# Attention and expert layer on one core: small VectorE steps that read at most one SBUF operand, and three kinds of work moved to other engines

## The chip, the cores and the metric

The kernel runs on one core of a Trainium2 chip. The core has TensorE (PE, matrix multiplication), VectorE (DVE), ScalarE (ACT), GpSimd (POOL) and SyncE (SP, which here only issues transfers), a working memory SBUF, and PSUM, into which TensorE writes. The metric is the device time of one execution in microseconds (us).

## What is computed

Sparse softmax attention, followed by a layer of eight experts, in float32. Per head, scores below the row's maximum minus tau are dropped. Each token then goes to the expert with the largest logit, up to a capacity per expert.

```
q, k, v: (4 batches, 8 heads, 576, 64);  w_gate: (512, 8);  w1: (8, 512, 1024);  w2: (8, 1024, 512)

scores = q @ k^T / 8
scores = where(scores >= max(scores) - tau, scores, -1e9)
attn   = exp(scores - max(scores));  attn /= sum(attn) + 1e-9
x      = concat of the heads of (attn @ v)              # (2304, 512)

logits = x @ w_gate;  e = argmax(logits);  gate_w = softmax(logits)[e]
out[i] = gate_w[i] * relu(x[i] @ w1[e]) @ w2[e]         # while expert e has room (576 tokens)
```

## The kernel before

Two heads make a pair; there are 16 pairs, four per batch. A head has 576 rows: four blocks of 128 and a tail of 64. Products need more than f16 gives, so q, k, v and the probabilities are split into an f16 high half and an f16 low half (the rest), and the products of halves are added up in PSUM.

For one pair, the stages are these, with the names that the profile shows for the tiles:

- Loads of q, k and v go to `qr`, `kr` and `v`. ScalarE scales q and k in place (L704, from the third pair on). `emit_hi` (L710, ScalarE) writes the high half into `qn` or `kn`; `emit_dup` (L714, VectorE) copies it to a second place of the same tile; `emit_lo` (L721, GpSimd; in the first two pairs VectorE) writes the low half. A transposing transfer makes `qT` and `kT` of them (L743, L748).
- v is scaled in place by GpSimd (`emit_vs`, L729); ScalarE makes the high half `vH` (L732) and GpSimd the low half `vL` (L735).
- Score pass: TensorE writes scores into two PSUM tiles `s` in turn (L761), and VectorE takes the row maximum of each (`emit_max`, L788, L790, L794) into `mx`. A score matmul waits until the maximum of the tile two before is taken.
- Threshold: `emit_m` (L799 to L804, six VectorE steps on 128x9 elements) makes of the maxima the two columns of `qn` that carry the row's threshold. A transposing transfer of `qn` follows (L753).
- Second pass: TensorE computes the transposed scores less the threshold into two PSUM tiles `d` (L761); ScalarE takes the exponential (L846), and VectorE multiplies it by "score is at or above the limit" (`emit_keep`, L850). The result lies in a part of the buffers that the profile names `w1b` and `w2b`.
- Of the five tiles per pair four are split into halves `p`: high by ScalarE (`emit_h16`, L816), low by `emit_l16` (L820). Of these four, tile 4 is VectorE's (`BY_V = {4}`) and the other three are GpSimd's.
- Output: TensorE multiplies the probabilities by v into the PSUM tile `xo` (`emit_av`, L866, L878); a column of constants in v gives the row sums in the same product. `xo` holds one head at a time in columns 0 to 259, and the tail rows behind them. ScalarE copies it to `xs` (`emit_xe`, L893); VectorE adds 1e-9 to the sums (`emit_r`, L899) and takes the reciprocal `rc` (L900); GpSimd multiplies (`emit_xm`, L914). The next head's output matmuls wait for `emit_xe`.
- After the fourth pair of a batch come transposes, logits, the choice of expert and scatters of the rows to DRAM. When all pairs are through, the expert part loads the weights, splits them into halves, and multiplies.

`ps_g`, which the profile names `gp`, is one PSUM bank that several small results share: transposed rows in columns 0 to 255, logits and ranks behind them, two 64-wide tail products at 320 and 384.

The order of the instructions is not the order of the text. Each step is a task with an engine, a duration, its dependencies and a due time (`T(name, engine, duration, function, dependencies, due)`), and a planner places the tasks one after the other on each engine by these durations and due times; each engine then runs its list in order. The due times are offsets to the pair's number (`PR`). The planner's duration of `emit_m`, for example, is 600 ns, and that of `emit_l16` 2350 ns on GpSimd and 1130 ns on VectorE.

## Time and profile before

| | |
|---|---|
| median of 3 runs | 714.22 us (709.1 to 725.44) |
| the profiled execution | 712.3 us, span 710.4 us |
| busy: TensorE / VectorE / ScalarE / GpSimd | 584.7 / 530.8 / 339.1 / 333.1 us |
| attention up to about 422 us, expert part behind | |
| granted TensorE clock, middle of the attention (120 to 340 us) | 0.90 of full |

An instruction's busy time runs from its start to its end, so it holds whatever the instruction itself waits for after it has begun. Idle time before an instruction is put down to the event that released it. Matmuls overlap each other, so a busy TensorE is not one at its peak.

### The profile page before, as it was taken

What the parts mean: (1) busy time and instruction counts of PE and PEld (TensorE: products, weight loads), DVE (VectorE), ACT (ScalarE), POOL (GpSimd) and SP (SyncE); (2) the same over time, 40 slices, a digit from 0 to 9 for tenths busy, and PEclk for the clock granted to TensorE, in tenths of its full rate; (3) what the DMA queues carried; (4) which work ended last, traced back from release to release, by engine and by line L of the source; (5) the groups of instructions that cost most, each with busy time, mean ns of one, the idle gap of its engine ahead of it and who ended that gap; (6) DMA issues with size and microseconds to landing.
All of it is one profiled execution on the core that took longest, in us unless ns stands there. A gap on an engine that the chain in (4) does not pass through costs nothing.

```text
span 710.4 us, 15942 instructions
## 1 busy us (share of the span) xinstructions
PE 584.7 (82%) x5990; PEld 389.1 (55%) x5990; DVE 530.8 (75%) x989; ACT 339.1 (48%) x535; POOL 333.1 (47%) x323
## 2 busy tenths in 40 slices
PE   0668877797798888878976886689999699899993
PEld 0225644575556665545744683577586268558741
DVE  5678988979999989999799767755456557686552
ACT  2347565546556655555344745446664206324300
...
GB/s 159 178 164 119 118 118 89 80 118 147 90 116 109 135 79 133 101 88 65 51 77 52 212 120 214 176 247 107 315 266 182 222 64 152 176 245 79 140 189 83
DMA packets 172428, 98.97 MB, mean 139 GB/s; under 512 B 147123, under 2 KB 159479, under 8 KB 172346
## 3 DMA queue, kind: packets, MB, share of 16 engines
...
q10 hardware_dynamic: 1296, 0.89, 0.4%
...
## 4 chain that ended last, share of the span: by engine, by line
PE 30%; DVE 30%; DMA 15%; issue 13%; POOL 4%; ACT 4%; SPq 3%; POOLq 0%; ACTq 0%; DVEq 0%
DVE w2b L850 7%; DVE mx L788 6%; DMA ws<-in_moe_w_dram 5%; PE s L761 5%; PE xo L866 4%; PE d L761 4%; PE b L370 4%; DVE rc L899 3%; PE b L377 3%; PE gp L930 2%; PE b L413 2%; PE gp L413 2%; POOL out_dram L602 2%; DMA latey<-xd,gix 2%; PE xo L413 2%
## 5 line engine op out<-in xcount | busy, mean ns | idle before, releaser
L761 PE MATMUL s<-kT,qT 128*128 128x512 f16 (+2 forms) x576 | 108.7, 330 | 67.5 <-DVE mx L788 46.5
L850 DVE SCALAR_TENSOR_TENSOR w2b<-d,ntau,w2b 128x1024 f32<-128x1024 f32 x80 | 101.8, 1273 | 9.0 <-ACT w2b L846 8.9
L788 DVE TENSOR_REDUCE mx<-s 128x1 f32<-128x512 f32 x144 | 95.0, 677 | 16.5 <-PE s L761 16.1
L294 POOL DMA_DIRECT2D ws<-in_moe_w_dram x50 | 36.9, 738 | 148.9 <-DVE w1b L307 68.7
L761 PEld LDWEIGHTS <-qT 128*128 128x128 f16 (+1 forms) x640 | 41.0, 108 | 98.9 <-issue 71.3
L846 ACT ACTIVATE w2b<-d 128x1024 f32<-128x1024 f32 x80 | 79.9, 1020 | 31.0 <-PE d L761 30.1
L761 PE MATMUL d<-qT,kT 128*128 128x512 f16 (+2 forms) x576 | 88.0, 317 | 6.6 <-DVE w2b L850 6.1
L377 PE MATMUL b<-w1b,latex 128*128 (+2 forms) x816 | 80.6, 277 | 5.1 <-issue 5.0
L820 POOL TENSOR_TENSOR p<-w2b,p 128x1024 f16<-128x1024 f32 x31 | 66.1, 2134 | 27.9 <-ACT p L816 27.5
L377 PEld LDWEIGHTS <-latex 128*128 128x128 f16 (+1 forms) x816 | 63.2, 102 | 20.4 <-issue 4.2
L761 PEld LDWEIGHTS <-kT 128*128 128x128 f16 (+1 forms) x640 | 39.6, 107 | 50.8 <-issue 27.4
L866 PE MATMUL xo<-v,w2b 128*128 128x65 f32 x256 | 56.5, 304 | 0.0
L816 ACT ACTIVATE p<-w2b 128x1024 f16<-128x1024 f32 x42 | 44.2, 1052 | 24.8 <-DVE w2b L850 24.5
L413 PEld LDWEIGHTS <-lateh 128*128 128x128 f16 (+1 forms) x408 | 31.3, 105 | 42.2 <-issue 10.7
L307 DVE SCALAR_TENSOR_TENSOR w2b<-ws,w2b 128x1024 f16<-128x1024 f32 (+1 forms) x40 | 39.5, 1006 | 19.1 <-ACT w2b L305 16.6
L370 PEld LDWEIGHTS <-w1b 128*128 128x128 f16 x768 | 46.6, 102 | 9.1 <-issue 7.6
L370 PE MATMUL b<-earlyx,w1b 128*128 128x128 f16 x768 | 49.9, 225 | 1.7 <-DVE earlyx L352 1.6
L866 PEld LDWEIGHTS <-p 128*128 128x128 f16 x1008 | 45.3, 104 | 10.4 <-issue 2.5
L307 DVE SCALAR_TENSOR_TENSOR w1b<-ws,w1b 128x1024 f16<-128x1024 f32 (+1 forms) x40 | 40.0, 1007 | 12.0 <-ACT w1b L305 12.0
L866 PE MATMUL xo<-vH,p 128*128 128x65 f16 x672 | 48.2, 201 | 0.1
L305 ACT ACTIVATE w2b<-ws 128x1024 f16<-128x1024 f32 (+1 forms) x40 | 34.3, 880 | 25.6 <-DMA ws<-in_moe_w_dram 23.8
L305 ACT ACTIVATE w1b<-ws 128x1024 f16<-128x1024 f32 (+1 forms) x40 | 34.1, 882 | 25.4 <-DMA ws<-in_moe_w_dram 25.4
...
## 6 DMA issues: line engine op xcount, KB each, us to landing
...
```

Of the source, the lines that this page charges most:

```text
L305: nc.scalar.activation(out=dst[:, :, 0, :], in_=t, func=AF.Copy, scale=W_SCALE)
L307: nc.vector.scalar_tensor_tensor(out=dst[:, :, 1, :], in0=t, scalar=W_SCALE, in1=dst[:, :, 0, :], op0=ALU.mult, op1=ALU.subtract)
L370: nc.tensor.matmul(out=hp[:, f * P:(f + 1) * P], lhsT=wb[0][:, o:o + P], rhs=xT[t][:, xi], start=(d == 0 and z == 0), stop=(d == NB - 1 an ...
L377: nc.tensor.matmul(out=hp[m, 0:FC], lhsT=xT[t][:, xi, m], rhs=wb[0][:, bass.ds(r + (2 * d + wi) * FC, FC)], start=(d == 0 and z == 0), sto ...
L413: nc.tensor.matmul(out=yp[m], lhsT=h[:, o, hi, m], rhs=wb[1][:, bass.ds(r + wi * DM, DM)], start=(z == 0), stop=(z == len(ops) - 1),)
L761: nc.tensor.matmul(out=out, lhsT=l, rhs=r, start=(z == 0), stop=(z == 1), **kw)
L788: V.tensor_reduce(out=m[:, 0, i:i + 1], in_=ps_s[i % 2], axis=AX.X, op=ALU.max)
L816: nc.scalar.activation(out=p16_of(s, k)[:, 0], in_=p32_of(s, k), func=AF.Copy)
L820: eng.tensor_tensor(out=p[:, 1], in0=p32_of(s, k), in1=p[:, 0], op=ALU.subtract)
L846: nc.scalar.activation(out=t, in_=d, func=AF.Exp, scale=sc_s)
L850: V.scalar_tensor_tensor(out=t, in0=d, scalar=ntau, in1=t, op0=ALU.is_ge, op1=ALU.mult)
L866: nc.tensor.matmul(out=ps_x[:, j * DV:j * DV + r.shape[-1]], lhsT=l, rhs=r, start=(z == 0), stop=(z == len(ops) - 1))
```

## The change

The maxima of a pair go to a tile of another layout: `mx` is now `[P, KB, 2]` (KB = 9), with the two maxima of a row side by side, and one reduction over the last axis takes the place of the elementwise maximum. It is done twice, once into PSUM (`a`) and once into SBUF (`m`, in the new tile `mm`). The following steps keep their intermediate values in PSUM, in 27 columns of `ps_g` from column 448 on (54 with the next pair), so that each step has at most one tensor operand in SBUF. `emit_r` reads the row sums from the PSUM tile `xo` instead of from `xs`. `emit_dup` is gone: `emit_hi` writes both places in one ScalarE instruction that reads its input twice. The scaling of v moves from GpSimd to ScalarE. The low half of tile 4 moves from VectorE to GpSimd. The tasks' durations and dependencies follow; the due times are the same.

```diff
-        mxs = [right.tile([P, 4, KB], F32, name=f"mx{i}") for i in range(2)]
+        mxs = [right.tile([P, KB, 2], F32, name=f"mx{i}") for i in range(2)]
+        mms = [right.tile([P, KB], F32, name=f"mm{i}") for i in range(2)]
...
-            nc.scalar.activation(out=n[:, 0, :, 0:D], in_=raw, func=AF.Copy, scale=sc)
-
-        def emit_dup(s, is_q):
-            n = qns[s % NQN] if is_q else kns[s % NKN]
-            V.tensor_copy(out=n[:, 1, :, 0:D] if is_q else n[:, 0, :, D:], in_=n[:, 0, :, 0:D])
+            out = view(n[:, 0, 0], [[KB * P if is_q else D, 2], [P, KB], [1, D]])
+            src = view(raw[:, 0], [[0, 2], [D, KB], [1, D]])
+            nc.scalar.activation(out=out, in_=src, func=AF.Copy, scale=sc)
...
-            nc.gpsimd.tensor_scalar(out=v, in0=v, scalar1=QK_SCALE, scalar2=None, op0=ALU.mult)
+            nc.scalar.activation(out=v, in_=v, func=AF.Copy, scale=QK_SCALE)
...
-                V.tensor_reduce(out=m[:, 0, i:i + 1], in_=ps_s[i % 2], axis=AX.X, op=ALU.max)
+                V.tensor_reduce(out=m[:, i, 0:1], in_=ps_s[i % 2], axis=AX.X, op=ALU.max)
...
-            m, n = mxs[s % 2], qns[s % NQN]
-            V.tensor_tensor(out=m[:, 2], in0=m[:, 0], in1=m[:, 1], op=ALU.max)
-            V.scalar_tensor_tensor(out=m[:, 3], in0=m[:, 2], scalar=-1.0, in1=m[:, 2], op0=ALU.mult, op1=ALU.max)
-            V.tensor_scalar(out=m[:, 3], in0=m[:, 3], scalar1=ROUND, scalar2=ntau, op0=ALU.mult, op1=ALU.add)
-            V.scalar_tensor_tensor(out=m[:, 3], in0=m[:, 3], scalar=0.0, in1=m[:, 2], op0=ALU.max, op1=ALU.subtract)
-            V.tensor_scalar(out=n[:, 1, :, D], in0=m[:, 3], scalar1=1.0 / MC, scalar2=None, op0=ALU.mult)
+            m, n = mms[s % 2], qns[s % NQN]
+            o = CM + s % 2 * 3 * KB
+            a, w, g = (ps_g[:, o + i * KB:o + (i + 1) * KB] for i in range(3))
+            for out in (a, m):
+                V.tensor_reduce(out=out, in_=mxs[s % 2], axis=AX.X, op=ALU.max)
+            V.scalar_tensor_tensor(out=w, in0=a, scalar=-1.0, in1=m, op0=ALU.mult, op1=ALU.max)
+            V.tensor_scalar(out=w, in0=w, scalar1=ROUND, scalar2=ntau, op0=ALU.mult, op1=ALU.add)
+            V.scalar_tensor_tensor(out=g, in0=w, scalar=0.0, in1=m, op0=ALU.max, op1=ALU.subtract)
+            V.tensor_scalar(out=n[:, 1, :, D], in0=g, scalar1=1.0 / MC, scalar2=None, op0=ALU.mult)
             V.scalar_tensor_tensor(
-                out=n[:, 1, :, D + 1], in0=n[:, 1, :, D], scalar=-MC, in1=m[:, 3], op0=ALU.mult, op1=ALU.add
+                out=n[:, 1, :, D + 1], in0=n[:, 1, :, D], scalar=-MC, in1=g, op0=ALU.mult, op1=ALU.add
             )
...
-            V.tensor_scalar(out=r0, in0=t[:, :, D:], scalar1=1e-9 * QK_SCALE, scalar2=None, op0=ALU.add)
+            sums = ps_x[rows, o:o + n * DV].rearrange("p (j d) -> p j d", d=DV)[:, :, D:]
+            V.tensor_scalar(out=r0, in0=sums, scalar1=1e-9 * QK_SCALE, scalar2=None, op0=ALU.add)
...
-        BY_V = {4}
+        BY_V = set()
...
-                T(("hi" + n, s), "A", 660, partial(emit_hi, s, is_q, scaled), got + free, u + PR["hi"] + is_q)
-                T(("du" + n, s), "V", 220, partial(emit_dup, s, is_q), [("hi" + n, s)], u + PR["lo"] + is_q)
+                T(("hi" + n, s), "A", 1170, partial(emit_hi, s, is_q, scaled), got + free, u + PR["hi"] + is_q)
...
-            T(("vs", s), "G", 1800, partial(emit_vs, s), [("lv", s)], u + PR["vs"])
+            T(("vs", s), "A", 760, partial(emit_vs, s), [("lv", s)], u + PR["vs"])
...
-                        need += [("xe", s, 0)] if x == 1 else last("xe", s - 1, 1 if x == 0 else 2)
+                        need += [(m, s, 0) for m in ("xe", "r")] if x == 1 else last("xe", s - 1, 1 if x == 0 else 2) + last("r", s - 1, 1 if x == 0 else 2)
...
-                T(("r", s, x), "V", 200, partial(emit_r, s, x), [("xe", s, x)], t1 + PR["xe"])
+                T(("r", s, x), "V", 200, partial(emit_r, s, x), [("av", s, x, j) for j in js], t1 + PR["xe"])
```

The first place in the order is VectorE's list around the threshold chain of one pair in the middle of the attention. Before, it reads (`s_144` and `s_145` are the two score tiles, `rc_192` the row sums of the second head):

```order
L794 TENSOR_REDUCE mx_186<-gp 128x1
L899 TENSOR_SCALAR rc_192<-xs_189 128x4
L900 RECIPROCAL rc_192<-rc_192 128x4
L799 TENSOR_TENSOR mx_186<-mx_186 128x9
L800 SCALAR_TENSOR_TENSOR mx_186<-mx_186 128x9
L801 TENSOR_SCALAR mx_186<-mx_186,ntau 128x9
L802 SCALAR_TENSOR_TENSOR mx_186<-mx_186 128x9
L803 TENSOR_SCALAR qn_178<-mx_186 128x9
L804 SCALAR_TENSOR_TENSOR qn_178<-qn_178,mx_186 128x9
L788 TENSOR_REDUCE mx_187<-s_144 128x1
L788 TENSOR_REDUCE mx_187<-s_145 128x1
L714 COPY kn_175<-kn_175 128x9x64
```

The same place of the changed kernel, whose lines are numbered a little differently (L801 to L806 are the chain, L852 is `emit_keep`, L903 the row-sum step):

```order
L793 TENSOR_REDUCE mx_186<-gp 128x1
L801 TENSOR_REDUCE gp<-mx_186 128x9
L801 TENSOR_REDUCE mm_188<-mx_186 128x9
L802 SCALAR_TENSOR_TENSOR gp<-gp,mm_188 128x9
L803 TENSOR_SCALAR gp<-gp,ntau 128x9
L804 SCALAR_TENSOR_TENSOR gp<-gp,mm_188 128x9
L805 TENSOR_SCALAR qn_178<-gp 128x9
L806 SCALAR_TENSOR_TENSOR qn_178<-qn_178,gp 128x9
L852 SCALAR_TENSOR_TENSOR w2b<-d_146,ntau,w2b 128x1024
L852 SCALAR_TENSOR_TENSOR w2b<-d_147,ntau,w2b 128x1024
L903 TENSOR_SCALAR rc_194<-xo 128x4
L904 RECIPROCAL rc_194<-rc_194 128x4
```

The chain has seven rows instead of six, the copy behind it is gone, and the row-sum step, which now reads `xo`, stands behind two large steps instead of ahead of the chain.

The second place is ScalarE's list at about the same time. Before (`w2b<-d` is the exponential, `p` and `w1b<-w2b` the high half of probabilities):

```order
L846 ACTIVATE w2b<-d_146 128x1024
L816 ACTIVATE p_157<-w2b 128x1024
L924 ACTIVATE w1b<-gp 128x256
L704 ACTIVATE kr_171<-kr_171 128x576
L924 ACTIVATE w1b<-gp 128x256
L816 ACTIVATE p_158<-w2b 128x1024
L846 ACTIVATE w2b<-d_147 128x1024
L846 ACTIVATE w2b<-gp 128x64
L710 ACTIVATE qn_178<-qr_173 128x9x64
L710 ACTIVATE kn_176<-kr_172 128x9x64
```

And in the changed kernel (L728 is the scaling of v, L713 the doubled copy, L848 the exponential, L818 the high half):

```order
L848 ACTIVATE w2b<-d_147 128x1024
L728 ACTIVATE v_167<-v_167 128x10x64
L713 ACTIVATE kn_175<-kr_171 128x2x9x64
L895 ACTIVATE xs_190<-xo 128x260
L818 ACTIVATE w1b<-w2b 128x1024
L848 ACTIVATE w2b<-d_146 128x1024
L848 ACTIVATE w2b<-d_147 128x1024
L713 ACTIVATE qn_177<-qr_174 128x18x64
L818 ACTIVATE w1b<-w2b 128x1024
```

The scaling of v, which waits for its load, and two instructions of twice the size now stand between the exponentials.

## Rows read from the trace of the kernel before

**Rows 1.** Page, 40 equal slices: span, busy tenths of TensorE and VectorE.
```profile
span 710.4 us, 15942 instructions
...
PE   0668877797798888878976886689999699899993
...
DVE  5678988979999989999799767755456557686552
```

**Rows 2.** Busy time by stretch: PE, PEld, DVE, ACT, POOL, clock, DMA, GB/s.
```profile
120.00:340.00 220.00, 186.83 (x2139) 127.00 (x2137) 205.24 (x365) 124.50 (x186) 135.03 (x110) 0.90 0.56 107
...
422.00:710.00 288.00, 252.81 (x2238) 167.57 (x2237) 169.75 (x314) 112.08 (x193) 82.72 (x95) 0.93 0.71 176
```

**Rows 3.** Waits, 120 to 340 us: total us, times, longest.
```profile
PE s L761 <- DVE mx L788: 28.9, 19, 3.4
```

**Rows 4.** Timeline of VectorE: start us, duration us; pairs 3 and 13.
```profile
91.56 0.14 DVE L799 TENSOR_TENSOR mx<-mx 128x9 f32<-128x9 f32 x1
...
327.03 0.14 DVE L799 TENSOR_TENSOR mx<-mx 128x9 f32<-128x9 f32 x1
```

**Rows 5.** Timeline of VectorE, 187 to 193 us.
```profile
187.18 1.27 DVE L850 SCALAR_TENSOR_TENSOR w2b<-d,ntau,w2b 128x1024 f32<-128x1024 f32 x1
...
188.50 0.89 DVE L899 TENSOR_SCALAR rc<-xs 128x4 f32<-128x4 f32 x1
...
190.72 2.09 DVE L803 TENSOR_SCALAR qn<-mx 128x9 f16<-128x9 f32 x1
```

**Rows 6.** Timeline of GpSimd, the same stretch.
```profile
187.23 2.13 POOL L820 TENSOR_TENSOR w1b<-w2b,w1b 128x1024 f16<-128x1024 f32 x1 [0.29 <-ACT w1b L816]
...
190.64 2.12 POOL L820 TENSOR_TENSOR w1b<-w2b,w1b 128x1024 f16<-128x1024 f32 x1
```

**Rows 7.** Groups of VectorE: busy us, mean ns; idle before.
```profile
L799 DVE TENSOR_TENSOR mx<-mx 128x9 f32<-128x9 f32 x16 | 6.0, 373 | 0.0
L800 DVE SCALAR_TENSOR_TENSOR mx<-mx 128x9 f32<-128x9 f32 x16 | 4.6, 286 | 0.6
L801 DVE TENSOR_SCALAR mx<-mx,ntau 128x9 f32<-128x9 f32 x16 | 9.7, 608 | 0.6
L802 DVE SCALAR_TENSOR_TENSOR mx<-mx 128x9 f32<-128x9 f32 x16 | 10.6, 660 | 0.6
L803 DVE TENSOR_SCALAR qn<-mx 128x9 f16<-128x9 f32 x16 | 9.9, 617 | 0.8 <-DMA kr<-in_k_dram 0.3
L804 DVE SCALAR_TENSOR_TENSOR qn<-qn,mx 128x9 f16<-128x9 f16 x16 | 10.5, 659 | 0.5
L899 DVE TENSOR_SCALAR rc<-xs 128x4 f32<-128x4 f32 (+1 forms) x48 | 30.8, 642 | 8.0 <-ACT xs L893 7.6
L714 DVE COPY qn<-qn 128x576 f16<-128x576 f16 x16 | 9.1, 568 | 4.2 <-ACT qn L710 4.2
L714 DVE COPY kn<-kn 128x576 f16<-128x576 f16 x16 | 7.3, 458 | 3.3 <-ACT kn L710 3.2
L820 DVE TENSOR_TENSOR p<-w2b,p 128x1024 f16<-128x1024 f32 x11 | 15.3, 1394 | 1.3 <-ACT p L816 1.1
```

**Rows 8.** Groups nearest to the changed kernel's steps, on three engines.
```profile
L794 DVE TENSOR_REDUCE mx<-gp 128x1 f32<-128x64 f32 x16 | 3.4, 211 | 0.0
L850 DVE SCALAR_TENSOR_TENSOR w2b<-gp,ntau,w2b 128x64 f32<-128x64 f32 x16 | 4.4, 272 | 0.7 <-ACT w2b L846 0.7
L710 ACT ACTIVATE kn<-kr 128x576 f16<-128x576 f32 x16 | 10.8, 679 | 3.5 <-DMA kT<-kn 3.4
L816 ACT ACTIVATE p<-w2b 128x1024 f16<-128x1024 f32 x42 | 44.2, 1052 | 24.8 <-DVE w2b L850 24.5 <-DVE bl L450 0.2
L820 POOL TENSOR_TENSOR p<-w2b,p 128x1024 f16<-128x1024 f32 x31 | 66.1, 2134 | 27.9 <-ACT p L816 27.5
```

**Rows 9.** The group of GpSimd's value scaling.
```profile
L729 POOL TENSOR_SCALAR v<-v 128x640 f32<-128x640 f32 x16 | 30.7, 1919 | 20.8 <-DMA v<-in_v_dram 20.8
```

**Rows 10.** The chain that ended last, at the end of the attention.
```profile
404.93 3.23 DVE rc L899
```

More of the change, by code (lines that the diff above doesn't have):

```diff
@@ L761, in cross @@
             nc.tensor.matmul(out=out, lhsT=l, rhs=r, start=(z == 0), stop=(z == 1), **kw)
-        CS, CD = 320, 384
+        CS, CD, CM = 320, 384, 448
         def emit_s(s, i):
@@ L897, in emit_r @@
         def emit_r(s, x):
-            t, r0, r1, _, n = xs_of(s, x)
-            V.tensor_scalar(out=r0, in0=t[:, :, D:], scalar1=1e-9 * QK_SCALE, scalar2=None, op0=ALU.add)
+            _, r0, r1, rows, n = xs_of(s, x)
+            o = TO if x == 2 else 0
+            sums = ps_x[rows, o:o + n * DV].rearrange("p (j d) -> p j d", d=DV)[:, :, D:]
+            V.tensor_scalar(out=r0, in0=sums, scalar1=1e-9 * QK_SCALE, scalar2=None, op0=ALU.add)
             V.reciprocal(out=r1, in_=r0)
@@ L1152, in attention_moe_kernel @@
                     free = [("zm", s)]
[L1153 to L1154 removed]
+                T(("hi" + n, s), "A", 1170, partial(emit_hi, s, is_q, scaled), got + free, u + PR["hi"] + is_q)
                 T(("lo" + n, s), "G" if scaled else "V", 1270 if scaled else 760, partial(emit_lo, s, is_q, scaled), [("hi" + n, s)], u + PR["lo"] + is_q)
                 users = [(m, s - NT, i) for m, c in (("s", CUT), ("d", 6)) for i in range(c)] if s >= NT else []
[L1157 removed]
+                T(("t" + n, s), "S", 0, partial(emit_turn_q if is_q else emit_turn_k, s), [("lo" + n, s)] + users, u + PR["tk"] + is_q, dma=2016, kind="turn")
             vfree = last("av", s - NV, 2, 0) + last("av", s - NV, 1, NJ - 1)
@@ L1315, in attention_moe_kernel @@
         busy = {b: [("swap_p",)] for b in range(2, 8)}
-        busy[0], busy[1] = [("xe", NPR - 1, 2)], [("most",), ("lim",)]
+        busy[0], busy[1] = [("xe", NPR - 1, 2), ("r", NPR - 1, 2)], [("most",), ("lim",)]
         T(("swap_p",), "X", 0, swap_p, [("p", NPR - 1, i) for i in range(6)] + [("max", NPR - 1, i) for i in SI], 0)
```

9 lines of the change are left out of this document (4 added, 5 removed).

## The prediction

> **What bounds the kernel now.** I read the page's slices first. VectorE's digits stand at 9 from about 120 to 340 us, the middle of the attention, and fall to 5 to 7 once the expert part runs; TensorE shows 7 to 9 in the attention and 9 at the end [rows 1]. So the attention has two candidates, and the table by stage splits them: from 120 to 340 us VectorE is busy 205.24 of 220 us (93%), TensorE 186.83, ScalarE 124.50, GpSimd 135.03 [rows 2]. In the expert part VectorE has 169.75 of 288 us and TensorE 252.81: nothing that the change touches decides there.
>
> The list of waits for 120 to 340 us says who waits for whom: TensorE stood idle 28.9 us before score matmuls, for VectorE's row maxima that free their PSUM tile [rows 3]. TensorE's whole idle time there is 33.2 us (220 - 186.83), so VectorE makes nearly all of it.
>
> The rate is read from the first step of the threshold chain (L799), once per pair: pair 3 at 91.56 us, pair 13 at 327.03 us, so 235.47 / 10 = 23.55 us per pair [rows 4]. The 220 us hold 9.34 pairs. Per pair that gives VectorE 22.0 us, TensorE 20.0, ScalarE 13.3, GpSimd 14.5, and 3.1 us in which TensorE waits for the maxima.
>
> What fills VectorE is the point. In the timeline near 190 us a step on 128x9 elements (L803) takes 2.09 us, from 190.72 to 192.81, while GpSimd's low-half subtraction runs from 190.64 to 192.76; the row-sum step L899 starts at 188.50 and ends at 189.39, and GpSimd's subtraction before ends at 189.36 [rows 5, 6]. A small step that meets a GpSimd instruction ends when that one ends. The large L850, which reads one operand from PSUM and one from SBUF, starts at 187.18 beside the same subtraction and takes its usual 1.27 us [rows 5, 6]. So what is slow is reading SBUF alone by certain steps, not VectorE as a whole.
>
> **The change part by part, per pair.** *Threshold chain.* Before: 373 + 286 + 608 + 660 + 617 + 659 = 3.20 us [rows 7]. After: seven steps, each with at most one SBUF tensor, most writing PSUM. Nothing in the trace is exactly that; nearest are a small reduce from PSUM, 211 ns, and a small step with a PSUM and an SBUF tensor, 272 ns; unheld SBUF steps of this size go down to 0.14 us in the timeline [rows 4, 8]. So 7 x 0.14 = 1.0 to 7 x 0.27 = 1.9 us; I take 7 x 0.211 = 1.48. *Row sums.* Three steps of 642 ns, 1.93 us, become three PSUM reads of 0.211, 0.63 us. *Doubled copies.* 568 + 458 = 1.03 us leave VectorE. *Low half of tile 4.* 1.39 us leaves VectorE [rows 7]. Together 3.20 + 1.93 + 1.03 + 1.39 - 1.48 - 0.63 = 5.44 us less: VectorE falls from 22.0 to 16.6 us per pair.
>
> The page "Perfetto Trace Analysis" of the Trainium skill (Optimizing Scalar/DVE Operations) speaks against these parts: a VectorE access to PSUM has about 65 ns more overhead than one to SBUF, and moving work between VectorE and GpSimd may not help since they share an SBUF read port. By the first the ten steps cost an estimated 0.65 us more than unheld SBUF steps, about what 211 against 140 ns shows; by the second the low half would win nothing and 1.39 us would come off the gain. The trace agrees with the second only for steps of the held kind: L850 beside GpSimd was not held.
>
> *What takes the work.* ScalarE's doubled copy has 1152 elements; from 679 ns for 576 and 1052 ns for 1024 the slope is 0.83 ns an element, so 1.16 us, +0.48 us each, +0.96 for q and k [rows 8]. The value scaling, 640 elements, is 0.73 us on the same line. ScalarE goes from 13.3 to 15.0 us. GpSimd loses a scaling of 1.92 us [rows 9] and gains a subtraction of 2.13 us [rows 8]: 14.7 us. Beside a 20 us period both additions are hidden by idle time of their engines: 10.2 us on ScalarE, 9.0 on GpSimd at the old rate, 5 after. If that cover fails, they cost up to 1.7 us per pair (a rival below). The wait for the value load moves too: GpSimd stood 20.8 us for it in the run, 1.3 us per pair [rows 9], and now ScalarE may stand there, with two exponentials or a doubled copy queued behind it, as the instruction order shows.
>
> *A new wait.* The row-sum step now reads the output PSUM tile, so the output matmuls of the next head wait for it as well as for ScalarE's copy. It stands in VectorE's queue behind up to two L850. I cost it at nothing, because ScalarE's copy of the same tile is waited for anyway and VectorE has 3 to 4 us of slack per pair; the rival on the slow side prices the other end.
>
> **The sum.** With VectorE at 16.6 us, TensorE is next with 20.0 us per pair of its own. Taking away its 3.1 us of waits for maxima gives 23.55 - 3.1 = 20.45. Its granted clock was 0.90 there [rows 2]; fewer gaps should return part: the 20.0 us would be 18.0 at 1.00 (186.83 x 0.90 / 9.34), and I take 0.45 us of these 2.0, since new small gaps will come from ScalarE and the transposes. So 20.0 us, 3.55 us less per pair. From pair 3 to pair 15 there are 12 steps: 42.6 us. The first three pairs I leave as they are: VectorE is not full there, its slices climb from 5 to 9 [rows 1]. At the end the chain holds a row-sum step of 3.23 us [rows 10], which becomes 0.2: 3.0 us. The last low half on GpSimd adds 2.13 - 1.39 = 0.7. In all 44.9 us. The profiled execution took 712.3 us (span 710.4), 1.9 below the median 714.22, inside the runs' own scatter: 712.3 - 44.9 = 667.4.
>
> **The rivals.**
> *TensorE gets its full clock.* Then 18.0 us per pair: 5.55 x 12 = 66.6, with the ends 68.9, so 643 us. For it: the expert part runs at a granted 0.93 with TensorE nearly full [rows 2]. Against it: VectorE's 16.6 and ScalarE's 15.0 us leave little room for in-order queues. 0.13.
> *ScalarE's queue takes the place of VectorE.* Each pair pays the added 1.7 us plus about 0.3 of the 1.3 us of load waits before exponentials that TensorE's next tiles need: period 22.0, 1.55 x 12 + 2.3 = 20.9, so 691 us. For it: the doubled copies stand between exponentials. Against it: 5 us of idle per pair. 0.18.
> *The steps stay held.* If a step with one SBUF tensor also waits for GpSimd, only copies and the low half go, 2.4 us of VectorE's 22.0: 2.4 x 12 = 28.8, so 684 us. L850 speaks against it. 0.04.
> *The gain is eaten in other queues* (the order of all engines is planned anew, with due times chosen for the old loads): 0.6 us per pair left, 705 us. 0.07.
> *Slower: the output tile is held by VectorE.* Two of the three output groups of a pair use the same columns and wait for a row-sum step; if each stands behind two L850, 2 x 1.27 = 2.5 us, the pair pays 5.0 us against 3.55 won, 1.45 x 12 = 17 us more: about 729 us. It decides from 1.8 us of wait per group on. For it: the order puts that step right behind two L850 in places. Against it: the copy by ScalarE waits similarly today and TensorE's list has no large wait for it. 0.04. The forecast itself has 0.54, with its own range 655 to 682.
>
> **How the numbers follow.** A measurement of this kernel tells about 2%, 14 us, from no change. Under 700 us lie the forecast, the full clock, the held steps and nearly all of the ScalarE rival: 0.87. Between 700 and 728 lie the eaten gain, a little of the ScalarE rival and half of the slow one: 0.10. Above: 0.03. The range runs from the full clock, 643, to 700, where the ScalarE rival with its load waits ends.
>
> **What would show it.** Right: the chain's steps all near 0.2 us with no value over 0.5; the row-sum step the same; VectorE near 80% busy in the middle stage and TensorE's waits for maxima down to a few us; pairs 20 us apart. Wrong: steps of 2 us that end with a GpSimd instruction; ScalarE waiting for the value load with exponentials behind it; output matmuls waiting for the row-sum step; pairs still 23 us apart although VectorE has idle time.

## The result and the profile after

| | before | after |
|---|---|---|
| median, beside each other on one chip | 711.66 us | 665.22 us |
| ratio, 95% interval | | 0.9253 [0.9094, 0.9411] |
| the profiled execution / its span | 712.3 / 710.4 us | 658.05 / 656.3 us |
| start of the chain of pair 3 | 91.56 us | 80.75 us |
| pair 3 to pair 15 | 291.11 us | 248.64 us |
| from there to the end | 327.7 us | 326.9 us |

The changed kernel is 7.5% faster. Its four executions took 654.6 to 683.92 us, and the ratio leaves out those that lie more than 1.5% above the kernel's own shortest. The spans differ by 54.1 us: 10.8 before pair 3, 42.5 in the twelve pairs behind it, 0.8 in the rest. The marks do not cut TensorE's work at the same place, though: 538 of its 5990 matmuls had started by the mark of pair 3 before, and 477 by the same mark now. Counted from the 538th matmul to the 3337th, which began at the mark of pair 15 before, the stretch took 290.9 us and takes 242.1; in front of it 2.3 us are won and behind it 2.9. So the start wins less than its mark says and the twelve pairs more.

The page of the changed kernel, with the digits of TensorE and VectorE that answer to [rows 1]:

```profile
span 656.3 us, 15955 instructions
...
PE   0667989999799998999796968799999999889992
...
DVE  4657978888677797877968587453558575647452
```

VectorE's row of nines in the middle is gone, and the digits of TensorE there are mostly 9. The busy time by stretch gives the amounts (pairs 3 to 13, then the expert part; the columns are those of [rows 2]):

```profile
80.75:281.33 200.58, 187.07 (x2345) 128.84 (x2341) 159.38 (x369) 151.96 (x218) 147.16 (x121) 0.97 0.67 128
375.00:656.00 281.00, 248.11 (x2158) 162.29 (x2156) 165.68 (x300) 109.36 (x187) 82.78 (x95) 0.94 0.73 180
```

The same ten pairs of the kernel before:

```profile
91.56:327.03 235.47, 197.80 (x2288) 133.28 (x2287) 217.30 (x390) 134.97 (x203) 146.01 (x119) 0.91 0.55 106
```

Ten pairs take 200.58 us, so 20.06 each, where they took 23.55. VectorE is busy 15.9 us of a pair (79%), ScalarE 15.2 (76%), GpSimd 14.7, and TensorE 18.7 (93%). The bound has passed from VectorE to TensorE. TensorE's busy time per pair fell too, from 19.8 us, although 54 more matmuls started in the stretch (2338 after 2284); one matmul takes 80.0 ns of busy time on the mean where it took 86.6. The granted clock of the stretch is 0.97, so nearly all at the upper of its two levels, 2.4 GHz, against 0.91.

The first step of the chain at pairs 3 and 13, in the timeline of VectorE, answers to [rows 4]; between them a stretch in which GpSimd's subtraction runs beside the chain answers to [rows 5]:

```profile
80.75 0.18 DVE L801 TENSOR_REDUCE gp<-mx 128x9 f32<-128x18 f32 x1
...
119.62 0.18 DVE L801 TENSOR_REDUCE gp<-mx 128x9 f32<-128x18 f32 x1
...
120.12 0.23 DVE L803 TENSOR_SCALAR gp<-gp,ntau 128x9 f32<-128x9 f32 x1
...
120.91 0.15 DVE L903 TENSOR_SCALAR rc<-xo 128x4 f32<-128x4 f32 x1
...
281.33 0.17 DVE L801 TENSOR_REDUCE gp<-mx 128x9 f32<-128x18 f32 x1
```

The timeline of GpSimd at that time, as in [rows 6]:

```profile
118.39 4.27 POOL L822 TENSOR_TENSOR p<-w2b,p 128x1024 f16<-128x1024 f32 x2 [0.23 <-ACT p L818]
```

Two subtractions run from 118.39 to 122.66, and the whole chain and a row-sum step pass beside them at their usual 0.15 to 0.23 us. Nothing ends with the GpSimd instruction any more. The groups of VectorE say that it is so in all 16 pairs: the longest of all steps of the chain takes 0.24 us and the longest row-sum step 0.16, although between 6 and 12 of the 16 steps of each line begin while GpSimd runs an instruction. They answer to [rows 7]:

```profile
L904 DVE RECIPROCAL rc<-rc 128x4 f32<-128x4 f32 (+1 forms) x48 | 8.2, 172 | 2.9
L903 DVE TENSOR_SCALAR rc<-xo 128x4 f32<-128x4 f32 (+1 forms) x48 | 7.5, 157 | 18.7 <-ACT xs L895 10.5 <-PE xo L868 5.2 <-PE xo L880 2.7
...
L803 DVE TENSOR_SCALAR gp<-gp,ntau 128x9 f32<-128x9 f32 x16 | 3.8, 235 | 0.6
...
L805 DVE TENSOR_SCALAR qn<-gp 128x9 f16<-128x9 f32 x16 | 3.2, 198 | 0.5
L806 DVE SCALAR_TENSOR_TENSOR qn<-qn,gp 128x9 f16<-128x9 f16 x16 | 3.1, 195 | 0.5
...
L802 DVE SCALAR_TENSOR_TENSOR gp<-gp,mm 128x9 f32<-128x9 f32 x16 | 2.8, 175 | 0.5
L804 DVE SCALAR_TENSOR_TENSOR gp<-gp,mm 128x9 f32<-128x9 f32 x16 | 2.8, 174 | 0.6
L801 DVE TENSOR_REDUCE gp<-mx 128x9 f32<-128x18 f32 x16 | 2.8, 174 | 1.7 <-PE gp L760 1.6
L801 DVE TENSOR_REDUCE mm<-mx 128x9 f32<-128x18 f32 x16 | 2.6, 165 | 0.0
```

The seven means of the chain add up to 1.32 us per pair (3.20 before), and the three row-sum steps to 0.47 (1.93 before). The groups of ScalarE that took work over answer to [rows 8, 9]:

```profile
L713 ACT ACTIVATE kn<-kr 128x1152 f16<-128x1152 f32 x16 | 18.4, 1156 | 0.1
...
L728 ACT ACTIVATE v<-v 128x640 f32<-128x640 f32 x16 | 11.7, 734 | 13.4 <-DMA v<-in_v_dram 13.4
```

The waits from 100 to 300 us (total, times, longest), where [rows 3] showed 28.9 us in 220:

```profile
ACT v L728 <- DMA v<-in_v_dram: 6.9, 6, 2.4
...
PE s L760 <- DMA qT<-qn: 4.6, 2, 3.7
...
ACT xs L895 <- DVE rc L903: 4.1, 7, 1.5
...
PE s L760 <- DVE mx L787: 2.4, 4, 0.8
...
PEld xo L880 <- ACT w2b L848: 1.4, 4, 0.4
```

TensorE hardly waits for the maxima any more. Two waits that the change brought in are there and small: ScalarE for the value load, and ScalarE's copy of the output tile for the row-sum step.

### The profile page after: what moved, and what is told of

Its sections match the earlier page's. It is cut to its first block, busy times and chain, and to the rows that moved or that the text cites. A ratio compares the mean times of both kernels' runs of the same rounds, so it can differ in the third digit from the quotient of the medians.

```text
span 656.3 us, 15955 instructions
## 1 busy us (share of the span) xinstructions
PE 565.5 (86%) x5990; PEld 380.5 (58%) x5990; DVE 448.3 (68%) x957; ACT 363.0 (55%) x551; POOL 329.9 (50%) x323
## 5 line engine op out<-in xcount | busy, mean ns | idle before, releaser
L760 PE MATMUL s<-kT,qT 128*128 128x512 f16 (+2 forms) x576 | 99.3, 309 | 38.4 <-DMA kT<-kn 25.4
L852 DVE SCALAR_TENSOR_TENSOR w2b<-d,ntau,w2b 128x1024 f32<-128x1024 f32 x80 | 101.5, 1277 | 8.0 <-ACT w2b L848 7.8
L822 POOL TENSOR_TENSOR p<-w2b,p 128x1024 f16<-128x1024 f32 x42 | 89.6, 2134 | 20.0 <-ACT p L818 19.5
L760 PE MATMUL d<-qT,kT 128*128 128x512 f16 (+2 forms) x576 | 86.6, 303 | 5.9 <-DVE w2b L852 5.1
L848 ACT ACTIVATE w2b<-d 128x1024 f32<-128x1024 f32 x80 | 80.9, 1020 | 9.0 <-PE d L760 7.9
L760 PEld LDWEIGHTS <-qT 128*128 128x128 f16 (+1 forms) x640 | 39.6, 105 | 66.7 <-issue 29.0
L760 PEld LDWEIGHTS <-kT 128*128 128x128 f16 (+1 forms) x640 | 37.4, 103 | 47.9 <-issue 28.5
L413 PEld LDWEIGHTS <-lateh 128*128 128x128 f16 (+1 forms) x408 | 30.9, 103 | 42.5 <-issue 10.2
L307 DVE SCALAR_TENSOR_TENSOR w1b<-ws,w1b 128x1024 f16<-128x1024 f32 (+1 forms) x40 | 45.5, 1146 | 13.4 <-ACT w1b L305 13.4
L307 DVE SCALAR_TENSOR_TENSOR w2b<-ws,w2b 128x1024 f16<-128x1024 f32 (+1 forms) x40 | 39.8, 1006 | 18.7 <-ACT w2b L305 18.5
L370 PEld LDWEIGHTS <-w1b 128*128 128x128 f16 x768 | 47.3, 102 | 8.2 <-issue 6.0
L822 POOL TENSOR_TENSOR w1b<-w2b,w1b 128x1024 f16<-128x1024 f32 x22 | 46.9, 2134 | 8.7 <-ACT w1b L818 8.5
L818 ACT ACTIVATE p<-w2b 128x1024 f16<-128x1024 f32 x42 | 44.3, 1054 | 10.9 <-DVE w2b L852 10.6
L868 PEld LDWEIGHTS <-p 128*128 128x128 f16 x1008 | 43.7, 102 | 10.8 <-issue 1.7
```

The costliest lines, as they stand in the source:

```text
L307: nc.vector.scalar_tensor_tensor(out=dst[:, :, 1, :], in0=t, scalar=W_SCALE, in1=dst[:, :, 0, :], op0=ALU.mult, op1=ALU.subtract)
L370: nc.tensor.matmul(out=hp[:, f * P:(f + 1) * P], lhsT=wb[0][:, o:o + P], rhs=xT[t][:, xi], start=(d == 0 and z == 0), stop=(d == NB - 1 an ...
L413: nc.tensor.matmul(out=yp[m], lhsT=h[:, o, hi, m], rhs=wb[1][:, bass.ds(r + wi * DM, DM)], start=(z == 0), stop=(z == len(ops) - 1),)
L760: nc.tensor.matmul(out=out, lhsT=l, rhs=r, start=(z == 0), stop=(z == 1), **kw)
L818: nc.scalar.activation(out=p16_of(s, k)[:, 0], in_=p32_of(s, k), func=AF.Copy)
L822: eng.tensor_tensor(out=p[:, 1], in0=p32_of(s, k), in1=p[:, 0], op=ALU.subtract)
```

## The experiments

All numbers per pair are from the profiled execution of each kernel: ten pairs, from the first step of the chain of pair 3 to that of pair 13. "Behind 15" runs from the chain of pair 15 to the end of the span. The ratio is to the kernel before in the same call. Kernels E start from the kernel before and take one part of the change; kernels U start from the changed kernel and undo one part; A are the changed kernel itself. E1 and U1 keep the order of instructions on the other engines; in the other kernels the planner places the tasks anew, so what they show of a part includes that new order.

The kernels E, then A0, U1, U3 and P1, then the rest were run in three calls. The kernel before took 729.43, 711.52 and 725.19 us in them (medians), but its one profile is of an earlier call (714.22 us). Differences in "period" and "3 to 15" between E and before therefore compare two calls; only the ratios compare within one.

| kernel | ratio [interval] | period | VectorE per pair | pair 3 at | 3 to 15 | behind 15 |
|---|---|---|---|---|---|---|
| before | | 23.55 | 21.7 | 91.56 | 291.1 | 327.7 |
| after | 0.9253 [0.9094, 0.9411] | 20.06 | 15.9 | 80.75 | 248.6 | 326.9 |
| E1 chain | 0.9597 [0.9509, 0.9685] | 22.23 | 20.0 | 89.33 | 272.0 | 331.9 |
| E2 chain, row sums | 0.9633 [0.9535, 0.9731] | 21.44 | 18.6 | 89.83 | 265.7 | 339.8 |
| E3 copies, value scaling | 0.9701 [0.9567, 0.9835] | 23.33 | 21.2 | 85.14 | 284.1 | 331.1 |
| E4 low halves | 0.9782 [0.9693, 0.9871] | 22.12 | 20.3 | 86.60 | 276.3 | 347.0 |
| A0 | 0.9335 [0.9210, 0.9461] | 20.22 | 15.9 | 79.92 | 250.6 | 321.9 |
| U1 old chain | 0.9573 [0.9450, 0.9696] | 21.19 | 17.4 | 80.95 | 260.6 | 326.2 |
| U3 value scaling | 0.9493 [0.9367, 0.9619] | 20.32 | 16.4 | 80.54 | 253.5 | 338.7 |
| P1 five steps more | none | 20.58 | 17.3 | 79.78 | 258.3 | 340.6 |
| U2 low half | 0.9383 [0.9303, 0.9464] | 20.16 | 17.3 | 84.36 | 252.2 | 332.6 |
| U4 row sums | 0.9330 [0.9236, 0.9423] | 20.46 | 17.9 | 80.75 | 255.2 | 323.9 |
| A1 | none | 20.56 | 16.0 | 79.75 | 255.5 | 343.0 |
| U3 again | none | 20.35 | 16.3 | 80.55 | 251.6 | 347.3 |

A1 and U3 again have no ratio on record: their executions took 657.43 to 683.58 us and 662.9 to 681.19, the profiled ones 680.01 and 681.19. P1 was run once. For E3 and E4 a gain is shown, but not that it is above 2%. In pairs 3 to 15 the unaltered kernel itself took 248.6, 250.6 and 255.5 us.

**E1, the threshold chain alone.** The row sums, the copies and the low half stay as before; the order on all engines is that of before.

```diff
...
-            V.tensor_tensor(out=m[:, 2], in0=m[:, 0], in1=m[:, 1], op=ALU.max)
...
+            for out in (a, m):
+                V.tensor_reduce(out=out, in_=mxs[s % 2], axis=AX.X, op=ALU.max)
...
```

> The kernel before with the threshold chain alone of the change; the planner's tasks and so the order of every engine stay as before. Theory (small steps on SBUF operands are held by GpSimd, and VectorE sets the rate): the chain's steps fall from 3.20 us per pair to 7 x 0.19 = 1.3, VectorE from 22.0 to about 20.1 us, and the pair from 23.6 to about 21.9 us; over 12 pairs 20 us, ratio about 0.97. Rival (the gain comes from the newly planned order, not from the steps): with the old order the ratio is 0.99 to 1.01. Rival (what frees TensorE is the chain alone): pairs at 20.5 us, ratio 0.945.

Measured: period 22.23, 19.1 us won in pairs 3 to 15. VectorE loses 1.7 us per pair and the period 1.3. The row sums, which stayed in SBUF, are still held: 760 ns on the mean of 48. With the old order the ratio is 0.9597, so the rival that the gain is the newly planned order fell.

**E2, the chain and the row sums.** E1 and, besides,

```diff
...
-            V.tensor_scalar(out=r0, in0=t[:, :, D:], scalar1=1e-9 * QK_SCALE, scalar2=None, op0=ALU.add)
...
+            sums = ps_x[rows, o:o + n * DV].rearrange("p (j d) -> p j d", d=DV)[:, :, D:]
+            V.tensor_scalar(out=r0, in0=sums, scalar1=1e-9 * QK_SCALE, scalar2=None, op0=ALU.add)
...
```

> The kernel before with the threshold chain and the row sums read from PSUM. Theory: the row-sum step falls from 642 ns to 157, another 1.45 us per pair; VectorE at 18.6 us falls below TensorE's 20.0, so the pair comes to about 20.8 us and the ratio to 0.945 to 0.955, most of the whole gain. Rival (the output tile waits for VectorE): slower than the chain alone, ratio 0.97 to 0.99.

Measured: another 6.4 us in pairs 3 to 15, but the ratio did not move (0.9633 against 0.9597, each inside the other's interval). In the profiled execution the stretch behind pair 15 is 7.9 us longer than that of E1, which takes the gain back; whether it was so in the others is not known. The expectation missed, in the period (20.8) and in the ratio; the last two runs below are about that stretch.

**E3, doubled copies and value scaling on ScalarE.**

```diff
-            nc.scalar.activation(out=n[:, 0, :, 0:D], in_=raw, func=AF.Copy, scale=sc)
...
-        def emit_dup(s, is_q):
...
+            nc.scalar.activation(out=out, in_=src, func=AF.Copy, scale=sc)
...
-            nc.gpsimd.tensor_scalar(out=v, in0=v, scalar1=QK_SCALE, scalar2=None, op0=ALU.mult)
+            nc.scalar.activation(out=v, in_=v, func=AF.Copy, scale=QK_SCALE)
...
```

> The kernel before with the doubled copies and the value scaling on ScalarE alone; chain, row sums and low halves as before. Theory: 1.03 us of VectorE's 22.0 per pair go, and GpSimd reads SBUF 1.9 us less per pair, so the held steps shrink a little: pair at 22.3 us, 12 x 1.2 = 15 us, ratio about 0.98. Rival (ScalarE pays for the longer copies and the value load): ratio 1.00 or more.

Measured: period 23.33, 7.0 us won in pairs 3 to 15, and pair 3 begins 6.4 us earlier than in before. The period missed the expected 22.3: VectorE lost only 0.5 us per pair of the 1.03. Its low half of tile 4, which reads two SBUF tensors, took 2.02 us on the mean of 11 pairs where it took 1.39 [rows 7], so part of the time came back there. ScalarE did not make the kernel slower, so that rival fell.

**E4, all low halves on GpSimd.**

```diff
-        BY_V = {4}
+        BY_V = set()
...
-                    T(("l16", s, c), e, 1130 if e == "V" else 2350, partial(emit_l16, s, c, nc.vector if e == "V" else nc.gpsimd), [("h16", s, c)], pr + PR["l"])
+                    T(("l16", s, c), e, 1130 if e == "V" else 2150, partial(emit_l16, s, c, nc.vector if e == "V" else nc.gpsimd), [("h16", s, c)], pr + PR["l"])
```

The planner's duration of the other low halves goes with it, from 2350 to 2150 ns.

> The kernel before with all low halves on GpSimd alone. Theory: VectorE loses 1.46 us per pair, but GpSimd subtracts 2.13 us longer per pair, and each small step still on SBUF is held more often: some 0.15 of its held time comes back (2.13 of 14.5 us more), 0.6 us. Net 0.9 us per pair, 10 us, ratio 0.985. Rival (the holding does not depend on what GpSimd runs): 1.46 x 12 = 17.5 us, ratio 0.975. Rival (GpSimd as bound): 1.00 or more.

Measured: VectorE 1.4 us less per pair, the period 1.4 us less, 14.8 us won in pairs 3 to 15. One for one, as a full engine answers. The expected 0.9 us per pair was too little: the held steps together take as long as before (chain 3.09 us per pair, row sums 1.72, copies 1.32; before 3.20, 1.93 and 1.03), so GpSimd's longer work did not lengthen them, as the first rival had it.

The four parts alone win 19.1 + 6.4 + 7.0 + 14.8 = 47.3 us in these pairs; together they win 42.5. Counted from the 538th matmul to the 3337th it is 52 us and 49. Nearly all of it adds up.

**A0, the changed kernel as a control.**

> The changed kernel once more, as the control that the others of this call are set against. Both theories: ratio 0.91 to 0.94 to the kernel before, pairs 20 us apart.

Measured: pairs 3 to 15 in 250.6 us, ratio 0.9335, the same result as the first time within the intervals.

**U1, the changed kernel with the old chain.** Only the rows of the chain differ, on VectorE alone.

```diff
...
-            for out in (a, m):
-                V.tensor_reduce(out=out, in_=mxs[s % 2], axis=AX.X, op=ALU.max)
...
+            V.tensor_tensor(out=m[:, 2], in0=m[:, 0], in1=m[:, 1], op=ALU.max)
...
```

> The changed kernel with the threshold chain as before (all operands in SBUF); the tasks are the same, so the order of every other engine is the changed kernel's, instruction for instruction. Theory (held steps, and VectorE now has slack): the chain's steps take 3 us per pair again; VectorE rises from 15.9 to some 17.8 us of a pair and stays below TensorE, so only the part that TensorE waits for returns: pairs 21.0 to 21.5 us, 1.02 times the changed kernel. Rival (VectorE is the bound whatever happens): the whole 1.9 us return, pairs at 22 us, 1.035 times. Rival (the gain of the chain was the planned order): 1.00 times.

Measured: period 21.19, 10.1 us more in pairs 3 to 15 than A0, ratio 0.9573 against 0.9335 (the intervals still touch). That is the theory's 21.0 to 21.5 us and 1.02; the order alone would have given A0's time. The groups of its chain:

```profile
L797 DVE TENSOR_TENSOR mx<-mx 128x9 f32<-128x9 f32 x16 | 10.9, 684 | 0.1
...
L798 DVE SCALAR_TENSOR_TENSOR mx<-mx 128x9 f32<-128x9 f32 x16 | 8.8, 547 | 0.6
...
L899 DVE TENSOR_SCALAR rc<-xo 128x4 f32<-128x4 f32 (+1 forms) x48 | 7.5, 156 | 18.2 <-ACT xs L891 10.2 <-PE xo L864 5.3 <-PE xo L876 2.5
```

The steps in SBUF are held again, the first worst (684 ns, against 373 in before [rows 7], where other steps took the hold). In the same run the row-sum step, which reads PSUM, keeps its 156 ns. So the hold belongs to the step's operands, not to the kernel. The waits in pairs 3 to 13 that grew, of A0:

```profile
ACT xs L895 <- DVE rc L903: 4.9, 9, 1.6
...
PE s L760 <- DVE mx L787: 2.3, 4, 0.9
```

and of U1:

```profile
ACT xs L891 <- DVE rc L899: 10.7, 10, 3.2
...
PE s L759 <- DVE mx L786: 5.3, 8, 2.0
```

The output path and the score matmuls both stand longer for VectorE, though its share is only 82% (173.51 of 211.88 us).

**U3, the value scaling on GpSimd again.**

```diff
-            nc.scalar.activation(out=v, in_=v, func=AF.Copy, scale=QK_SCALE)
+            nc.gpsimd.tensor_scalar(out=v, in0=v, scalar1=QK_SCALE, scalar2=None, op0=ALU.mult)
```

> The changed kernel with the scaling of v on GpSimd again. Theory (ScalarE and GpSimd both have a quarter of a pair idle, so this part is free): pairs at 20 us, 0.99 to 1.01 times the changed kernel. Rival (ScalarE stands for the load of v, 13.4 us in the run, and this reaches TensorE): faster, 0.985 times. Rival (GpSimd's 1.9 us more hold the rest back): 1.015 times.

Measured: 253.5 us in pairs 3 to 15, 2.9 more than A0 and less than A1 has; behind pair 15 16.7 us more, which became a question of its own. The ratio is 1.017 times that of A0, the number of the last rival, but what makes it lies behind pair 15 and not where steps are held.

**P1, which forms are held.** Five small steps more behind each chain, whose results nothing reads: a scaling from SBUF into PSUM (L811), the same within SBUF (L812), a maximum of two SBUF tensors into PSUM (L813) and into SBUF (L814), and a copy from PSUM to SBUF (L815).

```diff
...
+            V.tensor_scalar(out=w, in0=m, scalar1=0.5, scalar2=None, op0=ALU.mult)
+            V.tensor_scalar(out=pb[:, 0], in0=m, scalar1=0.5, scalar2=None, op0=ALU.mult)
+            V.tensor_tensor(out=a, in0=m, in1=pb[:, 0], op=ALU.max)
+            V.tensor_tensor(out=pb[:, 1], in0=m, in1=pb[:, 0], op=ALU.max)
+            V.tensor_copy(out=pb[:, 0], in_=w)
```

> The changed kernel with five more small VectorE steps (128x9 elements) behind each threshold chain, which write scratch only: a scaling from SBUF to PSUM, a scaling from SBUF to SBUF, a maximum of two SBUF tensors into PSUM, a maximum of two SBUF tensors into SBUF, and a copy from PSUM to SBUF. Theory (held are steps that read two tensors from SBUF, and scalings and copies that stay within SBUF): the first and the last never above 0.3 us, the other three up to 2 us where a GpSimd instruction runs. Rival (held is whatever reads SBUF alone): the first is held as well. Rival (held is whatever writes SBUF and reads SBUF): the third is not held. The time itself rises by some 5 x 0.2 us per pair and more where steps are held: 0 to 20 us.

Measured, in the timeline of VectorE at two pairs:

```profile
81.21 0.17 DVE L811 TENSOR_SCALAR gp<-mm 128x9 f32<-128x9 f32 x1
81.29 1.25 DVE L812 TENSOR_SCALAR pb<-mm 128x9 f32<-128x9 f32 x1
82.57 0.17 DVE L813 TENSOR_TENSOR gp<-mm,pb 128x9 f32<-128x9 f32 x1
...
312.50 0.16 DVE L812 TENSOR_SCALAR pb<-mm 128x9 f32<-128x9 f32 x1
312.70 1.98 DVE L813 TENSOR_TENSOR gp<-mm,pb 128x9 f32<-128x9 f32 x1
```

and of GpSimd at the same two:

```profile
80.39 2.12 POOL L829 TENSOR_TENSOR p<-w2b,p 128x1024 f16<-128x1024 f32 x1
...
312.49 2.16 POOL L829 TENSOR_TENSOR p<-w2b,p 128x1024 f16<-128x1024 f32 x1 [3.92 <-ACT p L825]
```

The first subtraction ends at 82.51. L811 and three chain steps before it start inside it and run unheld; L812, the same scaling with its result in SBUF, ends at 82.54. At the second pair L812 started 0.01 us after the subtraction, too near to tell which came first, and came through; L813, with two SBUF inputs, is then the one that lasts to the end of it (314.68; the subtraction ends at 314.65).

In eight of the 16 pairs both L811 and L812 start while GpSimd subtracts. L811 takes 171 ns each time; L812 ends within 0.04 us of the subtraction each time, after up to 1.67 us (mean of all 16: 731 ns, unheld 163). L813 meets a subtraction only in the one pair shown. L814 meets only the last 0.05 us of one, and L815 none, so these rows say nothing of the two. What is held is therefore not "a step that reads SBUF": it is a scaling from SBUF to SBUF, though it reads one tensor only, and a step with two SBUF tensors, for which L813 is one case and the old chain in U1 and [rows 7] more. Not held are a reciprocal from SBUF to SBUF (L904 above, longest 0.18 us, 32 of 48 begun while GpSimd ran), a reduction within SBUF (L801 into `mm`, longest 0.17, 11 of 16), and a scaling from PSUM to SBUF (L805, longest 0.20, 7 of 16).

The page "SBUF — State Buffer" of the Trainium skill (Who interferes with whom) says this beforehand: VectorE shares one pair of SBUF ports with GpSimd, takes it for a second SBUF input and for copies and scalings in a two-port mode, never for a reduction on trn2, and the later of two instructions waits for the whole of the earlier. The rows above agree, with steps of 1.25 and 1.98 us that last to the end of the subtraction.

**U2, the low half of tile 4 on VectorE again.**

```diff
-        BY_V = set()
+        BY_V = {4}
...
-                    T(("l16", s, c), e, 1130 if e == "V" else 2150, partial(emit_l16, s, c, nc.vector if e == "V" else nc.gpsimd), [("h16", s, c)], pr + PR["l"])
+                    T(("l16", s, c), e, 1130 if e == "V" else 2350, partial(emit_l16, s, c, nc.vector if e == "V" else nc.gpsimd), [("h16", s, c)], pr + PR["l"])
```

> The changed kernel with the low half of tile 4 on VectorE again. Theory (VectorE has room left, TensorE sets the period): VectorE goes from 15.9 to about 17.3 us per pair, still under TensorE's 18.7, so the period stays at 20.0 to 20.6 us (0 to 6 us over 12 steps) and the ratio to before at 0.925 to 0.945. Rival (VectorE's list decides by order, not by load: a low half of 1.4 us, held beside GpSimd, delays the maxima behind it): period 21 us or more, TensorE's waits for the maxima back over 8 us per 200, ratio 0.955 or more. Against both: if the low half was worth what the single edit gave on the old kernel (14.8 us in pairs 3 to 15), period 21.2 and ratio 0.95.

Measured: VectorE 17.3 us per pair, period 20.16, ratio 0.9383. These are the theory's numbers; the rival's 21 us did not come, and TensorE waits 1.7 us for the maxima in 202, where the rival had 8 in 200. The 1.4 us that were worth 14.8 us over twelve pairs on the old kernel (E4) are worth 1.7 us here beside A0. The mark of pair 3 comes 4.4 us later than in A0, but 527 matmuls have started by then instead of 471, so it is the mark that moved. A measure without marks is the start of the 3337th matmul: 336.3 us here, 332.4 in A0, 337.2 in A1, which was run in the same call. These runs cannot tell the low half's cost from nothing. The output matmuls do wait for the row-sum step here, 5.2 us in six times, the longest 1.8 us.

**U4, the row sums from SBUF again.**

```diff
...
-            V.tensor_scalar(out=r0, in0=sums, scalar1=1e-9 * QK_SCALE, scalar2=None, op0=ALU.add)
...
+            V.tensor_scalar(out=r0, in0=t[:, :, D:], scalar1=1e-9 * QK_SCALE, scalar2=None, op0=ALU.add)
...
```

> The changed kernel with the row sums read from SBUF again, after ScalarE's copy, so that output matmuls no longer wait for the row-sum step. Theory (the step is held again, but VectorE has room): the step takes 0.5 to 0.7 us on the mean instead of 0.157, with a longest of 2 us or more; VectorE 15.9 to about 17.3 us per pair; period 20.0 to 20.6, ratio 0.925 to 0.945, and the end of the attention up to 2 us longer if the last step is held. Rival (the wait that the new reading added costs something: ScalarE stood 4.1 us per 200 us behind the row sums): period 19.5 to 19.9, ratio 0.92 or less.

Measured: period 20.46, ratio 0.9330. Its group, and the longest of them:

```profile
L901 DVE TENSOR_SCALAR rc<-xs 128x4 f32<-128x4 f32 (+1 forms) x48 | 31.9, 664 | 16.0 <-ACT xs L895 15.8
```

```profile
320.55 2.10 DVE L901 TENSOR_SCALAR rc<-xs 64x2 f32<-64x2 f32 x1
```

The step is held again, 664 ns instead of 157, VectorE rises by 2.0 us per pair, and the time does not change by anything that can be told. The rival, that the new wait for the row sums had cost something, fell: without it the period is not shorter.

**A1 and U3 again: the stretch behind pair 15.**

> The changed kernel unaltered, once more, beside the next run. Both: pairs 3 to 15 in 248 to 251 us, ratio 0.925 to 0.935. The theory that the stretch behind pair 15 differs from execution to execution by a late load of expert weights: its length is 320 to 342 us, and it follows ScalarE's longest wait for such a load (under 7 us: up to 331; 9 us and more: 338 and up). The rival (the place of the value scaling sets it): 328 us or less here, whatever the loads do.

> The changed kernel with the value scaling on GpSimd, a second time. It gave 338.7 us behind pair 15 with a longest weight-load wait of 10.0 us, against 321.9 and 3.8 of the changed kernel. Theory (late loads come by chance of the execution): pairs 3 to 15 in 252 to 255 us again, behind them anywhere from 320 to 342, and 331 or less if the longest wait for a weight load is under 7 us; the ratio within 0.015 of the changed kernel's. Rival (GpSimd also issues the weight loads, and with the value scaling in its list it issues them later): 336 us or more again, a longest load wait of 9 us or more again, and a ratio 0.015 or more above the changed kernel's.

Measured: 343.0 us for the unaltered kernel, which had taken 321.9 and 326.9 in its two other profiles, with the same order of instructions. This profiled execution is among the kernel's longer ones (680.01 us), and its pairs 3 to 15 took 255.5 us, over the expected 248 to 251. U3 again has 251.6 us there and 347.3 behind. Busy time from pair 15 to the end, of A0 and of A1:

```profile
330.47:652.40 321.93, 284.61 (x2676) 194.03 (x2674) 196.31 (x364) 138.17 (x237) 111.57 (x119) 0.93 0.69 178
```

```profile
335.28:678.30 343.02, 290.80 (x2676) 196.96 (x2674) 191.85 (x364) 137.37 (x237) 112.43 (x119) 0.91 0.67 167
```

The instructions are the same in number; TensorE is busy 6.2 us longer at a lower granted clock (0.91 against 0.93) and idle 14.9 us longer. ScalarE's waits for the expert weights in that stretch, for A0, A1 and U3 again:

```profile
ACT w1b L305 <- DMA ws<-in_moe_w_dram: 22.3, 13, 3.8
```

```profile
ACT w1b L305 <- DMA ws<-in_moe_w_dram: 23.5, 11, 7.5
```

```profile
ACT w1b L305 <- DMA ws<-in_moe_w_dram: 39.6, 13, 10.1
```

The longest single wait is 3.8 to 6.6 us in A0, after, E1, E3, U1, U2, U4 and before, where the stretch takes 322 to 333 us; it is 7.5 to 11.6 in A1, P1, U3, U3 again and E4, where it takes 339 to 347. E2 is the exception, 339.8 us with a longest wait of 5.6. So the length of this stretch goes with a weight load that lands late; that the load causes it is not shown, and A1's 7.5 us lies between the two conditions that were set. The rival's 328 us or less did not hold for A1: the place of the value scaling does not decide it alone. Whether it adds to it stays open: both profiles of U3 waited 10 us for a load, as the second rival said, but the four executions of U3 again are not longer than those of A1. Why a load lands late was not tried.

## Why the prediction was right

The forecast was 667.4 us and 0.87 for faster; the median is 665.22. By its steps:

**The bound, right.** VectorE was full, and TensorE stood for its maxima. E4 shows it best: 1.4 us off VectorE took 1.4 us off the period. The wait of 28.9 us in 220 is down to 2.4 in 200.

**The chain and the row sums, right, slightly oversized.** 1.48 us was taken and 1.32 measured, 0.63 and 0.47 for the row sums. The bound from below, 0.14 us a step, came from unheld SBUF steps; the new chain's steps take 165 to 235 ns, hardly more. The low half was read from a group of 11; with the other five of the 16 pairs, 1.60 us each, it is 1.46 us and not 1.39. VectorE came to 15.9 us per pair, for a forecast of 16.6.

The page "Perfetto Trace Analysis" of the Trainium skill (Optimizing Scalar/DVE Operations), which spoke against the change, gives a VectorE access to PSUM an estimated 65 ns more than one to SBUF (about 125 against 60). Of the chain's two reductions, which read the same tile, the one that writes PSUM takes 174 ns and the one that writes SBUF 165, so on the side of the result these rows show 9 ns. Nor did the low half win nothing, which the prediction also drew from that page: it won 1.4 us per pair in E4.

**What took the work, right.** The copy was put at 1.16 us and took 1.156, the scaling at 0.73 and took 0.734; ScalarE 15.2 us for 15.0, GpSimd 14.7 for 14.7. ScalarE does stand for the value load, 6.9 us in 200, but TensorE's weight loads stand only 1.4 us of that stretch for an exponential: the rival of ScalarE's queue fell.

**The new wait at nothing, right for this kernel.** The wait that was priced, of output matmuls for the row-sum step, is not in the list of 100 to 300 us but for one weight load of 0.4 us. What is there was not named: ScalarE's copy and the row-sum step, which read the same tile, stand for each other (4.1 us for the step, the longest 1.5). U4, where the step reads SBUF again, is no faster. In U2, with more work on VectorE, the priced wait does appear, with 5.2 us and a longest of 1.8, the size from which the slow rival was to decide, but in six cases over ten pairs and not in every group.

**The period, right by the marks, undersized by the work.** 20.0 was forecast, 20.06 measured; 42.6 us over twelve pairs, 42.5 measured. That it agrees so closely is luck, because the marks moved: between the same matmuls the twelve pairs won 48.8 us. TensorE still idles 1.35 us per pair (200.58 - 187.07, over ten), more than half of it (7.4 of 13.5 us) for the transposing transfer of `qn`, which the prediction had among the small gaps to come. The term that was too small is the clock: 0.45 us of TensorE's 20.0 was to come back, and at 80.0 ns a matmul instead of 86.6 the 228 matmuls of an old pair take 1.5 us less.

**The start, wrong.** The failed step is "The first three pairs I leave as they are: VectorE is not full there". Before, pairs 2 and 3 lay 23.76 us apart, with VectorE busy 20.06 and TensorE idle for 4.3 us before score matmuls that waited for maxima; now they lie 14.8 us apart, and TensorE is busy throughout. A slice of the page is 17.8 us wide and averages over such a stretch. The two stretches, before (pairs 2 to 3) and after, and the wait before:

```profile
67.80:91.56 23.76, 19.49 (x226) 12.80 (x226) 20.06 (x34) 14.86 (x24) 16.36 (x12) 0.93 0.60 112
```

```profile
65.90:80.75 14.85, 14.85 (x200) 10.00 (x196) 13.73 (x30) 11.85 (x18) 11.80 (x11) 1.00 0.74 129
```

```profile
PE s L761 <- DVE mx L788: 4.3, 2, 3.8
```

How much it is worth cannot be read from the mark, which comes 10.8 us earlier, but after 61 matmuls fewer. Busy time from the start of the span to the mark before, to the mark now, and to the same number of matmuls now:

```profile
0.00:91.56 91.56, 58.03 (x538) 30.66 (x539) 65.36 (x133) 43.60 (x63) 52.84 (x68) 0.94 0.72 146
```

```profile
0.00:80.75 80.75, 49.26 (x477) 26.55 (x477) 53.14 (x122) 47.72 (x60) 41.89 (x63) 0.96 0.76 156
0.00:89.30 89.30, 55.00 (x538) 30.42 (x539) 57.92 (x136) 52.53 (x67) 46.11 (x66) 0.96 0.72 150
```

At the 538th matmul the changed kernel is 2.3 us ahead, at the 477th 5.4 (80.7 instead of 86.1 us); for A0 it is 1.1 and 6.0. So the step failed by 1 to 6 us. Which part counts there is open: the copies and the scaling alone (E3) bring the 538th matmul 5.8 us forward, the chain (E1) 1.3 and the low halves (E4) nothing, but with the low half back (U2) it comes 4.4 us earlier than in A0.

**The end, not to be settled by these runs.** 2.3 us were to be won behind pair 15 and 0.8 are seen (2.9 counted from the 3337th matmul), but this stretch of one and the same kernel took 321.9, 326.9 and 343.0 us. The held row-sum step of 3.23 us [rows 10] is gone in its kind: the longest now is 0.16 us.

**The total.** The sum was made against the profiled execution and gave 44.9 us; the two profiled executions differ by 54.3. Counted from the 538th matmul, the shortfall of 9.4 us lies for two thirds in the twelve pairs (48.8 won for 42.6) and for a quarter in the start. That the median still fell within 2.2 us of the forecast owes something to chance: two of the four executions are 14 to 26 us above the profiled one.

**What a part is worth in the changed kernel.** U1 and U2 put the same 1.4 us per pair back on VectorE (17.4 and 17.3). U2's ratio, 0.9383, lies within the intervals of the unaltered kernel, U1's, 0.9573, does not. The 3337th matmul starts at 343.5 us in U1, 11.1 later than in A0 of the same call, and at 336.3 in U2, 0.9 earlier than in A1 of the same call. The chain stands ahead of a row-sum step in VectorE's list and on the way from the maxima to the second score pass, and the low half does not. That its place makes the difference is argued, not shown: U2's order was planned anew, and from the 538th matmul to the 3337th both are slow (250.9 and 250.3 us; 242.0 in A0, 246.9 in A1).
